# Windowed value rows read once into SBUF, the overlap between windows copied on chip

## The chip, the cores and the metric

The kernel runs on one core of one Trainium2 chip. The metric is device time in microseconds (us) of that core; lower is better. Five engines work side by side, each with its own instruction stream that it executes in order: PE (TensorE, matmuls), DVE (VectorE), ACT (ScalarE), POOL (GpSimd) and SP (SyncE, which here only issues transfers). POOL, SP and ACT issue DMA transfers, each into a queue of its own; all of them are moved by the core's 16 DMA engines. An engine that reaches an instruction with a wait stands still until the wait is met.

## The reference

Two layers are computed one after the other.

```
# 1. chunked attention; B=4, H=8, S=768, D=64, 8 memory rows per head
for c in range(S // 32):                      # 24 chunks of 32 query rows
    window = rows [32c-16, 32c+40) of k and v, cut at 0 and S     # up to 56 rows
    k_full = concat(mem_k, k[window]);  v_full = concat(mem_v, v[window])
    out[chunk c] = softmax(scale * q_c @ k_full.T) @ v_full
# 2. x = out as [3072, 512]; 8 experts, F = 1024, top 2 by noisy logits
logits = x @ w_gate + log1p(exp(x @ w_noise)) * noise
y[token] = sum over its 2 best experts e of weight * relu(x @ w1[e]) @ w2[e]
```

Neighbouring windows overlap: rows 32 to 55 of the window of chunk c are rows 0 to 23 of the window of chunk c+1.

## The kernel before

**Stages.** An attention stage covers about the first 137 us of the profiled execution, with the top-2 routing woven in. From about 144 us on comes the expert stage, in which PE runs the experts' two matmuls over gathered tiles of 128 tokens (`mm1` L705, `mm2` L723) and results are scattered to DRAM (`put` L676). The expert stage can begin only when the last tile's routing is known.

**Tiling of attention.** A loop (L562) runs over 12 tiles t = 0 to 11, three for each of the 4 batches (`b, tp = divmod(i, TP)`). A tile is 256 tokens, in two halves of 128, with all 8 heads. Step i computes the scores of tile i+1 (`scores` L402: PE, then DVE for the maximum L423 and the subtraction L425), transposes the probabilities of tile i (`turn_p` L433: PE, then the ACT copy `pT` L439), stores the attention output of the batch before (`keep_x` L484, at tp = 0, issued from ACT's queue), transposes the output of tile i-1 (`turn_x` L466: PE, then the ACT copy `xT` L472), multiplies probabilities by values (`values` L442, PE L453, then DVE L460), takes the exponential for tile i+1 (`exps` L428, ACT L430), and computes the gate of tile i-1 (`gate` L475). PE, ACT, DVE and SP follow this hand-written order; on POOL the pinned instructions keep the program's order too.

**The values' way.** For each batch, `load_v` brings v into the SBUF buffer `vn` (cast to bf16), `spread_v` (L366, two POOL copies) reorders it into `vp`, and `window_v` (L372) does the rest. SP writes `vp` to a DRAM scratch `vd` (L374), padded by zero rows. POOL then issues two small transfers of the memory rows (L378) and four that read the windows back from `vd` (L383). The result `vb` holds, at each of 64 partitions of a half, one row of the window for all 24 chunks. The two halves of 64 partitions carry even and odd heads. In the buffer before, partitions 0 to 7 of a half hold memory rows and 8 to 63 the 56 window rows, read as rows 0 to 31 and rows 32 to 55. There are two `vb` buffers; batch b uses `vb[b % 2]`.

**What shares a tensor.** `vn`, the two `vb`, the buffers `nat` for the loaded k and q, and `xrow` (the attention output that `keep_x` stores) are all column ranges of one big SBUF tensor, `w_all`, which later holds the experts' weights. The program's planner derives waits between instructions from the regions of a tensor that they read and write.

**Order of POOL's queue.** For batch b+1, at step tp = 0 of batch b, POOL issues in this order: memory rows and windows of batch b+1 (L568), the loads of q and k of batch b+2 (L570), `spread_v(b + 2)`, and the load of v of batch b+3 (L573). Before the loop come v, k, q of batch 0, the windows of batch 0 (L528), then v, q, k of batch 1, its spread, and v of batch 2. The weights of experts 0 to 2 follow at steps 6 to 8.

Of the kernel before, what the change touches and what calls it, by code (L numbers as in the profile page):

```python
# [18 lines left out]
NEG = -1e30  # L19
# [3 lines left out]
def kernel(  # L23
# [24 lines left out]
    HP = H // 2  # L48
# [4 lines left out]
    NCH = S // CH  # L53
# [16 lines left out]
    def pin(i):  # L70
        tc.keep_in_program_order(i)
# [32 lines left out]
    def scratch(n):  # L104
        scol[0] -= n
        return wflat[:, scol[0]:scol[0] + n]
    xrow = [scratch(SO * Dm).rearrange("p (s r) -> p s r", s=SO) for _ in range(2)]
    vn = scratch(H * SO * D).rearrange("p (h c) -> p h c", h=H)
    vb = [scratch(2 * NCH * HP * D).rearrange("p (a c w) -> p a c w", a=2, c=NCH) for _ in range(2)][::-1]
    nat = [[scratch(H * SO * D).rearrange("p (h c) -> p h c", h=H) for _ in range(2)] for _ in range(2)]  # L110
    assert scol[0] >= 2 * WE
    mvs = w_all[0:B * NM, 0, 0:2 * H * D].bitcast(F32).rearrange("p (h d) -> p h d", h=H)
# [52 lines left out]
    mvn = keep.tile([B * NM, Dm], BF16, name="mvn")  # L165
# [53 lines left out]
    kT = keep.tile([128, HP, 2, SP], BF16, name="kT")  # L219
    qT = [keep.tile([128, HP, S], BF16, name=f"qT{i}") for i in range(2)]  # L220
    for par in range(2):
        nc.scalar.copy(vb[1][own(par), 1 - par].rearrange("p (x c) w -> p x (c w)", x=NCH // 2),
                       zeros[own(par), :].unsqueeze(1).to_broadcast([64, NCH // 2, Dm]))

    mkT = keep.tile([128, HP, 2, B * NM], BF16, name="mkT")
# [146 lines left out]
    def window_v(b):  # L372
        t, o = vb[b % 2], vd[b % 2]
        nc.sync.dma_start(out=o[LC:LC + S, :].rearrange("(p s) c -> p (s c)", s=SO), in_=vp)  # L374
        for par in range(2):
            p0 = par * 64
            cols = slice(par * 256, (par + 1) * 256)
            pin(nc.gpsimd.dma_start(out=t[p0:p0 + NM, par], in_=mvn[b * NM:(b + 1) * NM, cols].unsqueeze(1).to_broadcast([NM, NCH, 256])))  # L378
        for par in range(2):
            p0 = par * 64  # L380
            cols = slice(par * 256, (par + 1) * 256)
            for r0, n in ((0, CH), (CH, WIN - CH)):
                pin(nc.gpsimd.dma_start(out=t[p0 + NM + r0:p0 + NM + r0 + n, par],  # L383
                                        in_=o[r0:r0 + S, cols].rearrange("(c k) w -> k c w", k=CH)[0:n]))


    def turn(b, unit):
# [14 lines left out]
    def scores(t):  # L402
        b, tp = divmod(t, TP)
        ps_s = psS.tile([128, 2, HP, 2, KW], F32, name="ps_s")
        for j in range(2):
            for pair in range(HP):
                tk = (2 * tp + j) * 128
                nc.tensor.matmul(out=ps_s[:, j, pair, :, 0:NM], lhsT=qT[b % 2][:, pair, tk:tk + 128],
                                 rhs=mkT[:, pair, :, b * NM:(b + 1) * NM], start=True, stop=True)
        for j in range(2):  # L410
            for pair in range(HP):
                tk = (2 * tp + j) * 128
                for r in range(4):
                    tr = tk + r * CH
                    nc.tensor.matmul(out=ps_s[r * CH:(r + 1) * CH, j, pair, :, NM:KW], lhsT=qT[b % 2][:, pair, tr:tr + CH],  # L415
                                     rhs=kT[:, pair, :, tr:tr + WIN], start=True, stop=True, tile_position=(0, r * CH))
        if tp == 0:
            nc.vector.memset(ps_s[0:CH, 0, :, :, NM:NM + LC], NEG)
        if tp == TP - 1:
            nc.vector.memset(ps_s[128 - CH:128, 1, :, :, KW - RC:KW], NEG)  # L420
# [95 lines left out]
    with tc.manual_schedule(engines={ET.PE, ET.Activation, ET.DVE, ET.SP}):  # L516
# [5 lines left out]
        for par in range(2):  # L522
            nc.vector.tensor_copy(mkT[own(par), :, par, :], p_mk[own(par)].rearrange("p c x b m -> p c (x b m)"))
        for par in range(2):
            nc.vector.memset(vb[0][own(par), 1 - par], 0.0)
# [35 lines left out]
        r0, ra, rb, rc = Route(0, 6, 8), Route(6, 8, 8), Route(14, 6, 8), Route(20, 4, 4)  # L561
        for i in range(NT):  # L562
            b, tp = divmod(i, TP)
# [22 lines left out]
            if not last:  # L586
                sc = scores(i + 1)
# [291 lines left out]
    for i, (b, e, s0, ds_, n, ps_) in enumerate(steps):  # L879
        if i == 0:  # L880
# [5 lines left out]
            s0, n = 1, 2  # L886
# [11 lines left out]
        for pr in ps_:  # L898
            k = pairs.index(pr)
            x = pr.index(e)  # L900
# [8 lines left out]
        if i == 9:  # L909
# [3 lines left out]
            dstx, _, wx = next(dx), next(dx), next(dx)  # L913
# [21 lines left out]
    with tc.manual_schedule(engines={ET.Pool}):  # L935
        nov = nc.values_load(nxt[0:1, 0:1], min_val=0, max_val=NX,
                             skip_runtime_bounds_check_because="computed on chip from counts that sum to the tokens")
        with tc.If(nov > 1):
            for t in range(1, NX):
# [3 lines left out]
                dstx, _, wx = next(dx), next(dx), next(dx)  # L943
# [42 lines left out]
```

## Time and profile before

| what | value |
|---|---|
| median of 3 runs | 362.4 us (360.43 to 364.03) |
| the profiled execution's own time | 358.42 us |
| its span, and mean granted TensorE clock | 356.7 us, 0.867 |
| PE, DVE, ACT, POOL busy | 80%, 48%, 38%, 38% of the span |
| window reads L383 | 8 of 384 KB and 8 of 288 KB, median 13.0 and 13.3 us from issue to landing |
| writes of `vd` L374 | 4 of 768 KB, median 9.0 us |
| loads of v, k, q | 4 each of 768 KB, median 12.1, 20.9, 18.1 us |

Lines such as L383 are lines of the kernel before. "Landing" is when a transfer's completion arrives. A line of the timeline gives start, duration, engine, line, operation, how many instructions were merged (x8), and in square brackets how long the engine was idle before and whose completion ended that idle time. A letter q after an engine's name marks the engine's instruction queue (its sequencer) rather than its compute part.

### The profile page before, as it was taken

The page shows a single profiled execution, that of the slowest core. Times are in us where ns is not written, and L with a number is a line of the kernel's source. Part 1 is how long each engine was busy: PE and PEld are TensorE (multiplying, and loading weights), DVE is VectorE, ACT ScalarE, POOL GpSimd, SP SyncE. Part 2 cuts the span into 40 slices and gives each one's busy share as a digit, 9 for nine tenths or more (in the row PEclk, how much of TensorE's full clock was granted, in tenths as well). Part 3 has the DMA queues.
Part 4 walks back from the last instruction along what each step waited for, and adds up shares of the span by engine and source line. Part 5 has one row for each costly group of instructions (what it writes and reads, how often), then busy time and mean ns, then how long its engine had stood idle before and what let it go on. Part 6 is the DMA issues. An engine that isn't in the chain of part 4 may idle for free.

```text
span 356.7 us, 7042 instructions
## 1 busy us (share of the span) xinstructions
PE 285.9 (80%) x2934; PEld 186.3 (52%) x2955; DVE 170.3 (48%) x349; ACT 136.9 (38%) x189; POOL 134.3 (38%) x181
## 2 busy tenths in 40 slices
PE   0356577777847732999999999999999999999991
PEld 0245455666736621865544465664455775565540
DVE  7656456699689885531133302954310334223221
ACT  8813645564645610144322343213243222243310
POOL 6460573354453036706530744332580122201122
PEclk9995655565687865699999999999999999999998
DMA  8999999999999999499999999961289971100012
GB/s 122 235 171 169 245 174 208 251 198 211 247 156 208 253 249 180 106 194 143 178 196 235 209 173 252 159 119 51 87 166 189 208 184 54 53 2 2 25 47 81
DMA packets 49866, 56.97 MB, mean 160 GB/s; under 512 B 16931, under 2 KB 39523, under 8 KB 49828
## 3 DMA queue, kind: packets, MB, share of 16 engines
q0 software_dynamic: 34240, 46.82, 73.2%
q1 hardware_dynamic: 13920, 6.62, 10.9%
q10 hardware_dynamic: 1668, 3.02, 2.4%
q8 instruction: 25, 0.41, 0.5%
q14 instruction: 13, 0.11, 0.1%
HBM read 70.39 MB, written 13.96 MB: 236 GB/s over the span
## 4 chain that ended last, share of the span: by engine, by line
PE 33%; issue 20%; POOL 5%; DVE 4%; DMA 3%; POOLq 1%; ACT 0%; DVEq 0%
PE p_h L714 18%; PE p_y L726 13%; POOL out_dram L677 4%; DMA out_dram<-y,main_dst 1%; DMA xTt<-xt 1%; DMA xt<-xd,main_src 1%; POOL xt L671 1%; DVE w_all L460 1%; PE p_xt L691 0%; POOL w_all L844 0%; POOLq L981 0%; DVE mx L423 0%; DVE sc L425 0%; ACT xT L472 0%; PE ps_o L453 0%
## 5 line engine op out<-in xcount | busy, mean ns | idle before, releaser
L714 PE MATMUL p_h<-xTt,w_all 128*128 128x256 bf16 (+3 forms) x669 | 102.7, 313 | 0.7 <-DVE xTt L692 0.5
L726 PE MATMUL p_y<-w_all,h 128*128 128x512 bf16 x446 | 102.3, 379 | 0.9
L714 PEld LDWEIGHTS <-w_all 128*128 128x128 bf16 x736 | 70.0, 101 | 36.3 <-issue 0.7
L702 ACT ACTIVATE h<-p_h 128x512 bf16<-128x512 f32 (+1 forms) x81 | 44.7, 551 | 95.9 <-PE p_h L714 88.3
L726 PEld LDWEIGHTS <-h 128*128 128x128 bf16 x464 | 45.3, 98 | 51.6
L700 DVE TENSOR_SCALAR h<-p_h 128x512 bf16<-128x512 f32 (+1 forms) x49 | 31.0, 633 | 82.8 <-PE p_h L714 73.7
L677 POOL DMA_INDIRECT out_dram<-y,main_dst x28 | 30.9, 1103 | 87.9 <-DVE y L732 75.4
L732 DVE SCALAR_TENSOR_TENSOR y<-p_y,main_w,y 128x512 f32<-128x512 f32 x28 | 21.0, 750 | 39.2 <-PE p_y L726 32.5
L393 PE MATMUL p_t<-identb,w_all 128*64 128x128 bf16 x384 | 20.6, 288 | 23.0 <-DMA w_all<-in_k_dram 13.4
L671 POOL DMA_INDIRECT xt<-xd,main_src x28 | 27.9, 997 | 24.2 <-DMA xTt<-xt 13.0
L730 ACT ACTIVATE y<-p_y,main_w 128x512 f32<-128x512 f32 x28 | 19.2, 687 | 37.0 <-PE p_y L726 36.0
L393 PEld LDWEIGHTS <-w_all 128*64 128x64 bf16 x384 | 18.1, 155 | 25.2 <-DMA w_all<-in_k_dram 13.9
L439 ACT COPY pT<-p_p 128x1024 bf16<-128x1024 bf16 x12 | 12.1, 1012 | 27.5 <-PE p_p L436 27.5
L383 POOL DMA_DIRECT2D w_all<-vd x16 | 11.8, 747 | 23.8 <-DMA vd<-vp 19.3
L460 DVE TENSOR_TENSOR w_all<-ps_o,rs 128x512 bf16<-128x512 f32 x24 | 15.6, 686 | 8.2 <-PE ps_o L453 7.8
L415 PE MATMUL ps_s<-kT,qT 128*32 128x112 bf16 x384 | 11.6, 276 | 7.2 <-DVE kT L549 5.4
L368 POOL COPY vp<-w_all 128x1536 bf16<-128x1536 bf16 x8 | 11.5, 1469 | 13.2 <-DMA w_all<-in_v_dram 13.2
L430 ACT ACTIVATE pb<-sc 128x1024 bf16<-128x1024 f32 x12 | 12.8, 1063 | 8.9 <-DVE sc L425 8.7
L549 DVE COPY kT<-p_t 64x768 bf16<-64x768 bf16 x12 | 11.5, 955 | 7.9 <-PE p_t L393 7.8
L425 DVE TENSOR_TENSOR sc<-ps_s,mx 128x1024 f32<-128x1024 f32 x12 | 14.7, 1225 | 0.8
L423 DVE TENSOR_REDUCE mx<-ps_s 128x16 f32<-128x1024 f32 x12 | 14.7, 1224 | 0.8 <-PE ps_s L415 0.5
L453 PE MATMUL ps_o<-w_all,pT 128*32 128x128 bf16 x384 | 10.9, 280 | 3.3 <-issue 2.0
(172 smaller groups left out, 284.0 us busy)
## 6 DMA issues: line engine op xcount, KB each, us to landing
w_all<-in_moe_w_dram POOLq DMA_DIRECT2D x16, 1024.0 KB, 20.7
w_all<-in_moe_w_dram POOLq DMA_DIRECT2D x8, 512.0 KB, 13.8
w_all<-in_v_dram POOLq DMA_DIRECT2D x4, 768.0 KB, 12.1
w_all<-in_k_dram POOLq DMA_DIRECT2D x4, 768.0 KB, 20.9
w_all<-in_q_dram POOLq DMA_DIRECT2D x4, 768.0 KB, 18.1
vd<-vp SPq DMA_DIRECT2D x4, 768.0 KB, 9.0
w_all<-vd POOLq DMA_DIRECT2D x8, 384.0 KB, 13.0
w_all<-vd POOLq DMA_DIRECT2D x8, 288.0 KB, 13.3
```

The costliest lines, as they stand in the source:

```text
L393: nc.tensor.transpose(out=p_t[own(par), s, :], in_=src[:, 2 * pair + par, s * D:(s + 1) * D], identity=identb, tile_position=(0, par * 64))
L423: nc.vector.tensor_reduce(out=mx, in_=s3, axis=AX, op=Alu.max)
L425: nc.vector.tensor_tensor(out=sc, in0=s3, in1=bc(mx, KW), op=Alu.subtract)
L460: nc.vector.tensor_tensor(out=xr[:, j, 0:Dm].rearrange("p (h d) -> p h d", h=H), in0=ps_o[:, j].rearrange("p c a d -> p (c a) d"), in1=bc( ...
L671: i = nc.gpsimd.indirect_dma_start(out=xts[key].bitcast(I32), out_offset=None, in_=xd, in_offset=bass.IndirectOffsetOnAxis(ap=ix, axis=0))
L677: i = nc.gpsimd.indirect_dma_start(out=out, out_offset=bass.IndirectOffsetOnAxis(ap=ix, axis=0), in_=y, in_offset=None, bounds_check=N - 1 ...
L700: nc.vector.tensor_scalar(out=out_, in0=in_, scalar1=0.0, scalar2=None, op0=Alu.max)
L702: nc.scalar.activation(out=out_, in_=in_, func=Act.Relu)
L714: nc.tensor.matmul(out=o, lhsT=w(kp * F + f * 128, 128), rhs=x[:, kp], start=(kp == 0), stop=(kp == KP - 1))
L726: nc.tensor.matmul(out=p, lhsT=h[:, (f * n + j) * 128:(f * n + j + 1) * 128], rhs=w(KP * F + f * Dm, Dm), start=(f == 0), stop=(f == FB - 1))
L730: nc.scalar.activation(out=y, in_=p, func=Act.Copy, scale=weight)
L732: nc.vector.scalar_tensor_tensor(out=y, in0=p, scalar=weight, in1=y, op0=Alu.mult, op1=Alu.add)
```

## The change

The 64 partitions of a half of `vb` are now ordered as 56 window rows and then 8 memory rows; scores, masks and the memory transfer follow that order. `vb` has 25 chunk places instead of 24. Window rows 0 to 31 are read from `vd` for 25 chunks, by eight transfers per batch: for r = 0 to 3 and for each half, the eight rows r, r+4, ..., r+28, which go to every fourth partition. Rows 32 to 55 are no longer read from DRAM: SP's queue copies them from partitions 0 to 23, one chunk further on, one transfer for each half.

```
-    vb = [scratch(2 * NCH * HP * D).rearrange("p (a c w) -> p a c w", a=2, c=NCH) ...
+    vb = [scratch(2 * (NCH + 1) * HP * D).rearrange("p (a c w) -> p a c w", a=2, c=NCH + 1) ...
...
         for par in range(2):
-            pin(nc.gpsimd.dma_start(out=t[p0:p0 + NM, par], in_=mvn[...]...to_broadcast([NM, NCH, 256])))
+            pin(nc.gpsimd.dma_start(out=t[p0 + WIN:p0 + KW, par, 0:NCH],
+                                    in_=mvn[...]...to_broadcast([NM, NCH, 256])))
+        for r in range(4):
+            for par in range(2):
+                p0 = par * 64
+                cols = slice(par * 256, (par + 1) * 256)
+                pin(nc.gpsimd.dma_start(out=t[p0 + r:p0 + CH:4, par],
+                                        in_=o[:, cols].rearrange("(c k r) w -> r k c w", k=CH // 4, r=4)[r]))
         for par in range(2):
             p0 = par * 64
-            cols = slice(par * 256, (par + 1) * 256)
-            for r0, n in ((0, CH), (CH, WIN - CH)):
-                pin(nc.gpsimd.dma_start(out=t[p0 + NM + r0:p0 + NM + r0 + n, par],
-                                        in_=o[r0:r0 + S, cols].rearrange("(c k) w -> k c w", k=CH)[0:n]))
+            nc.sync.dma_start(out=t[p0 + CH:p0 + WIN, par, 0:NCH].rearrange("p c w -> p (c w)"),
+                              in_=t[p0:p0 + WIN - CH, par, 1:NCH + 1].rearrange("p c w -> p (c w)"))
...
-                nc.tensor.matmul(out=ps_s[:, j, pair, :, 0:NM], ...
+                nc.tensor.matmul(out=ps_s[:, j, pair, :, WIN:KW], ...
...
-                    nc.tensor.matmul(out=ps_s[r * CH:(r + 1) * CH, j, pair, :, NM:KW], ...
+                    nc.tensor.matmul(out=ps_s[r * CH:(r + 1) * CH, j, pair, :, 0:WIN], ...
```

The two masks (L418, L420) and the zeroing of `vb` (L222, L525) move by the same shifts.

More of the change, by code (lines that the diff above doesn't have):

```diff
@@ L108 @@
     vn = scratch(H * SO * D).rearrange("p (h c) -> p h c", h=H)
-    vb = [scratch(2 * NCH * HP * D).rearrange("p (a c w) -> p a c w", a=2, c=NCH) for _ in range(2)][::-1]
+    vb = [scratch(2 * (NCH + 1) * HP * D).rearrange("p (a c w) -> p a c w", a=2, c=NCH + 1) for _ in range(2)][::-1]
     nat = [[scratch(H * SO * D).rearrange("p (h c) -> p h c", h=H) for _ in range(2)] for _ in range(2)]
@@ L221 @@
     for par in range(2):
-        nc.scalar.copy(vb[1][own(par), 1 - par].rearrange("p (x c) w -> p x (c w)", x=NCH // 2),
+        nc.scalar.copy(vb[1][own(par), 1 - par, 0:NCH].rearrange("p (x c) w -> p x (c w)", x=NCH // 2),
                        zeros[own(par), :].unsqueeze(1).to_broadcast([64, NCH // 2, Dm]))
@@ L377, in window_v @@
             cols = slice(par * 256, (par + 1) * 256)
-            pin(nc.gpsimd.dma_start(out=t[p0:p0 + NM, par], in_=mvn[b * NM:(b + 1) * NM, cols].unsqueeze(1).to_broadcast([NM, NCH, 256])))
+            pin(nc.gpsimd.dma_start(out=t[p0 + WIN:p0 + KW, par, 0:NCH],
+                                    in_=mvn[b * NM:(b + 1) * NM, cols].unsqueeze(1).to_broadcast([NM, NCH, 256])))
+        for r in range(4):
[4 more added lines that the diff above has]
+                                        in_=o[:, cols].rearrange("(c k r) w -> r k c w", k=CH // 4, r=4)[r]))
         for par in range(2):
             p0 = par * 64
-            cols = slice(par * 256, (par + 1) * 256)
-            for r0, n in ((0, CH), (CH, WIN - CH)):
-                pin(nc.gpsimd.dma_start(out=t[p0 + NM + r0:p0 + NM + r0 + n, par],
-                                        in_=o[r0:r0 + S, cols].rearrange("(c k) w -> k c w", k=CH)[0:n]))
+            nc.sync.dma_start(out=t[p0 + CH:p0 + WIN, par, 0:NCH].rearrange("p c w -> p (c w)"),
+                              in_=t[p0:p0 + WIN - CH, par, 1:NCH + 1].rearrange("p c w -> p (c w)"))
     def turn(b, unit):
@@ L407, in scores @@
                 tk = (2 * tp + j) * 128
-                nc.tensor.matmul(out=ps_s[:, j, pair, :, 0:NM], lhsT=qT[b % 2][:, pair, tk:tk + 128],
+                nc.tensor.matmul(out=ps_s[:, j, pair, :, WIN:KW], lhsT=qT[b % 2][:, pair, tk:tk + 128],
                                  rhs=mkT[:, pair, :, b * NM:(b + 1) * NM], start=True, stop=True)
@@ L414, in scores @@
                     tr = tk + r * CH
-                    nc.tensor.matmul(out=ps_s[r * CH:(r + 1) * CH, j, pair, :, NM:KW], lhsT=qT[b % 2][:, pair, tr:tr + CH],
+                    nc.tensor.matmul(out=ps_s[r * CH:(r + 1) * CH, j, pair, :, 0:WIN], lhsT=qT[b % 2][:, pair, tr:tr + CH],
                                      rhs=kT[:, pair, :, tr:tr + WIN], start=True, stop=True, tile_position=(0, r * CH))
         if tp == 0:
-            nc.vector.memset(ps_s[0:CH, 0, :, :, NM:NM + LC], NEG)
+            nc.vector.memset(ps_s[0:CH, 0, :, :, 0:LC], NEG)
         if tp == TP - 1:
-            nc.vector.memset(ps_s[128 - CH:128, 1, :, :, KW - RC:KW], NEG)
+            nc.vector.memset(ps_s[128 - CH:128, 1, :, :, WIN - RC:WIN], NEG)
         s3 = ps_s.rearrange("p j c a w -> p (j c a) w")
@@ L524 @@
         for par in range(2):
-            nc.vector.memset(vb[0][own(par), 1 - par], 0.0)
+            nc.vector.memset(vb[0][own(par), 1 - par, 0:NCH], 0.0)
         nc.vector.tensor_copy(mvn.rearrange("m (a c d) -> m a c d", a=2, c=HP), mvs.rearrange("m (c a) d -> m a c d", a=2))
```

## The prediction

> **What bounds the kernel now.** The page first, then the stretches of the expert stage.
>
> ```profile
> PE 285.9 (80%) x2934; PEld 186.3 (52%) x2955; DVE 170.3 (48%) x349; ACT 136.9 (38%) x189; POOL 134.3 (38%) x181
> ...
> DMA  8999999999999999499999999961289971100012
> ```
> ```profile
> 160.00:180.00 20.00, 19.89 (x108) 10.62 (x109) 4.08 (x8) 8.15 (x15) 12.03 (x13) 1.00 1.06 163
> ```
>
> From 144 us on PE has no gap (19.89 of 20 us busy, clock 1.00), so whatever moves that stage's start moves the end by as much. Before it, the 16 DMA engines are full (16 slices of 8.9 us, 143 us, all but the first at 9) and PE is not. So I read the attention stage through its transfers. The timeline of POOL, which issues nearly all of them:
>
> ```profile
> 19.97 2.96 POOL L383 DMA_DIRECT2D w_all<-vd  x4 [4.95 <-DMA vd<-vp]
> 22.92 0.94 POOL L117 DMA_DIRECT2D w_all<-in_v_dram  x1
> 23.83 0.92 POOL L117 DMA_DIRECT2D w_all<-in_q_dram  x1
> 24.72 0.90 POOL L117 DMA_DIRECT2D w_all<-in_k_dram  x1
> 35.95 2.88 POOL L368 COPY vp<-w_all 128x1536 bf16<-128x1536 bf16 x2 [10.34 <-DMA w_all<-in_v_dram]
> ...
> 45.77 2.96 POOL L383 DMA_DIRECT2D w_all<-vd  x4 [4.42 <-issue]
> 48.72 0.92 POOL L117 DMA_DIRECT2D w_all<-in_q_dram  x1
> ```
>
> To see: right behind the four window reads the next loads are issued, so POOL's queue always holds a backlog, and its transfers land in the order of issue. The queue is what feeds PE and POOL. Now ACT around the first `keep_x` (L485), and PE behind it:
>
> ```profile
> 57.68 1.01 ACT L439 COPY pT<-p_p 128x1024 bf16<-128x1024 bf16 x1 [1.99 <-PE p_p L436]
> 57.76 0.37 ACTq L485 DMA_DIRECT2D xd<-w_all  x1
> 58.59 1.02 ACT L472 COPY xT<-p_x 128x1024 bf16<-128x1024 bf16 x1
> 59.49 1.07 ACT L430 ACTIVATE pb<-sc 128x1024 bf16<-128x1024 f32 x1
> ...
> 87.14 1.01 ACT L439 COPY pT<-p_p 128x1024 bf16<-128x1024 bf16 x1 [3.02 <-PE p_p L436]
> 87.22 0.34 ACTq L485 DMA_DIRECT2D xd<-w_all  x1
> 88.05 1.02 ACT L472 COPY xT<-p_x 128x1024 bf16<-128x1024 bf16 x1
> ```
> ```profile
> 68.03 1.49 PE L393 MATMUL p_t<-identb,w_all 128*64 128x128 bf16 x24 [2.63 <-DMA w_all<-in_q_dram]
> ```
>
> To see: ACT passes each `keep_x` at once, and its next copies follow within 1 us.
>
> **The change: what goes.** Per batch, 1,088 of 2,688 row pieces of 512 B are no longer read. The trace's landings give a full set after the memory rows 9.3 us (windows of batch 2: 77.5 to 86.9; of batch 3: 99.4 to 108.7), so 1,600 pieces are worth 5.5 us: 3.8 us less of queue per batch. POOL issues eight reads instead of four; at 0.72 us each (L383 takes 0.73 to 0.77, the smaller L378 0.67) that is 5.8 us instead of 2.96. The two copies of 24 x 12 KB on SP's queue are not in the trace. A 6 KB packet takes 247 ns and an engine gets few 12 KB rows, so 1 us of transfer; a small transfer (the gathers L671) lands 2.8 to 3 us after issue, the larger `vd` write 7.2 us. I take 3, between 2.8 and 7.2. Scores and masks only shift columns: nothing, as forms and counts stay.
>
> **What is added: waits.** The built program's own list of waits shows what the diff does not. The planner takes a write to every fourth partition as touching other columns of `w_all` too, so these appear, between buffers that share no byte:
> - window reads wait for the k, q and v loads issued before them (`nat`, `vn`);
> - the load of v (batch 1) and of q (batches 2, 3) waits for all eight window reads before it to land; behind it on POOL stand the other loads, the spread, the next windows;
> - `keep_x` of batches 0 and 1, on ACT, waits for all eight window reads of batch 2 and 3. Behind it on ACT stand the copy `xT` L472, the exponential L430 and the next `pT` L439; PE waits for each (gate, `turn_p`, `values`).
>
> The backlog that hid every transfer's latency is thus gone; how far 3.8 us per batch pays for it has to be added up.
>
> *POOL's chain, in us of the profiled execution.* A set of windows lands 8.3 after its start (seven issues of 0.72, then 3 for the last, small one). A load into an empty queue lands 8.1 after issue (v of batch 0: 1.5 to 9.6), one behind another +4.3 (k of batch 0: 9.56 to 13.84), or +5.9 where `vd` is written beside it (k of batch 1: 39.7 to 45.6).
> - windows 0 start at 20.3 (q of batch 0 lands 20.28; before 19.97), land 28.6 (before 32.7).
> - v1 28.6 + 8.1 = 36.7; q1 41.0; k1 46.9; v2 51.2 (before 35.9, 39.7, 45.6, 50.3).
> - windows 1 start at 51.2 (before 45.8), land 59.5, copied 62.5 (before 60.8).
> - q2 67.6; k2 73.5 beside the write of `vd`; v3 77.8 (before 68.0, 71.8, 76.2).
> - windows 2 start at 77.8, land **86.1** (before 86.9).
>
> So loads and windows come within about 2 us of where they came. This part alone costs about nothing: the saving pays for the lost backlog.
>
> *ACT's first hold.* The compute is about 1 us late by 58, so ACT arrives at `keep_x` at 58.8 and stands until 86.1. Then `xT` at 86.5, exponential to 88.4, scores (L415) and transposes on PE to 90.1, `pT` at 90.0 (before 64.59, +25.4). There the wait for q of 2.63 us (the PE line above) is gone, since q2 and k2 have landed: +22.9. From there to the next `keep_x` I see no idle time of PE put down to a transfer, so it keeps: `pT` at 110.0, `keep_x` reached at 110.1.
>
> *ACT's second hold.* The windows of batch 3 overwrite the buffer that `values` of tile 5 reads, and come behind POOL's `vals` (L342, before 81.84 to 83.66). That wait is old and hidden; now tile 5 is late. Its last values come at 81.9 + 22.9 = 104.8, `vals` ends by 106.0, memory rows 1.35, windows 3 start near 107 and land at 115.5. ACT goes on there: `xT` at 115.8 against 88.05, +27.7. Of this 0.3 comes back at q3 (PE idle 0.33). The 1.4 us idle at k3 does not come back: DVE, with the routing's `choose` and then the `kT` copies until 105.6, ends later there. The third `keep_x` waits for no window. Windows and copy 3 are landed by 119, before tile 9 needs them. Experts 0 and 1 follow by about 140, and expert 2, issued once `nat` is read (near 127), by about 150; the stage that needs them starts near 171.
>
> Sum: **+27 us** at the start of the expert stage, nothing after. On the profiled 358.4 us that is 385; this execution is 4.0 us under the median of 362.4 (360.4 to 364.0), and from the median it is 389. I give 388.
>
> **A rule against the change.** The nearest row for the new reads is the pair of memory-row transfers (eight partitions, one per half): issued 0.7 us apart, landed 21.52 and 21.89, and in batch 1 51.51 and 51.84, so the two overlap. The Trainium skill, DMA: Bandwidth & Descriptors, section Rules for kernel authors, says that transfers to two disjoint partition halves serialize and should be one transfer. By that rule the sum would be that of the second rival; the trace disagrees so far, in pairs of the same eight partitions.
>
> **The rivals.**
> 1. *PE and ACT catch up after the holds.* Everything loaded waits ready, and the clock in 50 to 70 us was granted at 0.50; at 1.00 a `turn_p` takes 0.62 instead of 1.03 us (both in the timeline). For: the stretch from 110 to 120 was at 0.91. Against: the clock is low where PE has gaps, and it keeps them. PE is busy 30 us in 60 to 100 (6.22, 7.98, 7.69 and 8.16 per 10 us, granted 0.50 to 0.76); a quarter of that, some 8 us, could go: +27 - 8 = +19, 381.
> 2. *Eight-partition reads do not overlap.* 25 pieces per engine at 9.3 x 16 / 2,688 = 55 ns are 1.4 us; eight in a row 11.1 us, a set 5.6 us longer than above. Three sets stand before the first hold's end and one before the second's: +27 + 22 = +49, 411. Against it: the pair above.
> 3. *Faster: the queue is all that matters.* If `keep_x` found its windows landed, ACT would not hold, and 3.8 us per batch would bring k of batch 3 (98.5 before) some 11 us earlier; half of that is lost to DVE's `choose`, leaving 5 to 8: 355. It decides at L485: windows 2 would have to land by 58.8, 27 us earlier than added up, though q2, k2 and v3 stand before them. Only waits that the program does not really carry would do it.
> 4. *Within 1%:* the hold is covered by waits that ACT would have had anyway. In 58 to 86 ACT's own waits on transfers are under 3 us; little.
>
> **How the numbers follow.** Forecast 0.74; rival 1 0.12; rival 2 0.06; rival 3 0.05; rival 4 0.03. The forecast's unknowns: the copies (up to +4 each, on no chain but beside q2 and v1), a set of windows 7.5 to 10, a load 7.5 to 9.5: the first hold ends between 81 and 97. That is 383 to 399; with 2 to 3 us for the second set and rival 1's 381, itself 5 us uncertain, 376 to 402; rivals 2, 3 and 4 are left out. A measurement of this kernel tells about 1% from no change (its three runs span 1%). Slower by over 1%: 0.74 + 0.12 + 0.06 = 0.92; within 0.03; faster 0.05.
>
> **What would show it.** In the changed kernel's profile: an idle of about 25 us on ACT before an `xT` copy, ended by window reads from `vd`, and a second of 4 to 7 us; two slices of PE near 0 at 65 to 86; the DMA row with digits under 9 in the first 100 us; v1 issued near 28.6, not 22.9; the first expert matmul (L714) near 171 instead of 144.14, and from there to the end the same 213 us. I am wrong if ACT passes L485 without a wait, if a set of windows takes over 10 us, or if the expert stage waits for weights.

## The result, and the profile after

The changed kernel takes 399.0 us (median of four runs, 397.6 to 400.4) against 361.6 us for the kernel before (360.4 to 364.0, measured beside it): a ratio of 1.103, with a 95% interval of 1.098 to 1.107. The prediction was 388 us, slower, with a range of 376 to 402. The profiled execution took 398.95 us, its span 397.2 us (before: 358.42 and 356.7). The profiled execution of before is thus 3.2 us faster than the median of its kernel, that of after is at its median; the two profiles differ by 40.5 us where the medians differ by 37.4.

First the page of the kernel after: busy shares, then PE and DMA in 40 slices of 9.9 us.

```profile
PE 284.2 (72%) x2955; PEld 183.3 (46%) x2955; DVE 169.9 (43%) x349; ACT 136.7 (34%) x189; POOL 143.2 (36%) x197
...
PE   0366483004552665437999999999998999999991
...
DMA  9949967957957999505999999996139991100012
```

PE does the same work (284.2 us busy, 285.9 before) in a longer span. Slices 7 and 8 of PE (counted from 0), 69.5 to 89.4 us, are nearly empty. The DMA row, full for 16 slices before, now has digits of 4 to 7 among the first 13: the queue runs dry although the kernel reads less (68.16 MB from HBM, 70.39 before).

The timeline of POOL shows why. L384 are now the window reads; they were L383.

```profile
21.00 5.20 POOL L384 DMA_DIRECT2D w_all<-vd  x8 [5.99 <-DMA w_all<-in_q_dram]
29.02 0.92 POOL L117 DMA_DIRECT2D w_all<-in_v_dram  x1 [2.83 <-DMA w_all<-vd]
...
39.08 2.88 POOL L368 COPY vp<-w_all 128x1536 bf16<-128x1536 bf16 x2 [7.37 <-DMA w_all<-in_v_dram]
...
53.97 5.17 POOL L384 DMA_DIRECT2D w_all<-vd  x8 [9.53 <-DMA w_all<-in_v_dram]
62.56 0.93 POOL L117 DMA_DIRECT2D w_all<-in_q_dram  x1 [3.42 <-issue]
...
85.11 5.17 POOL L384 DMA_DIRECT2D w_all<-vd  x8 [15.38 <-DMA w_all<-in_v_dram]
92.89 0.92 POOL L117 DMA_DIRECT2D w_all<-in_q_dram  x1 [2.61 <-DMA w_all<-vd]
```

In the square brackets two waits alternate that the kernel before did not have: window reads wait for a load (`in_q_dram`, `in_v_dram`), and the next load waits for the window reads (`vd`). Before, the loads followed the reads at once (22.92 behind 19.97). The line at 62.56 names no transfer as releaser ("issue"), but in the trace it too waits for the counters of these reads.

Now ACT around the first two `keep_x` (L490):

```profile
60.42 1.01 ACT L444 COPY pT<-p_p 128x1024 bf16<-128x1024 bf16 x1 [1.99 <-PE p_p L441]
92.47 0.37 ACTq L490 DMA_DIRECT2D xd<-w_all  x1
92.94 1.01 ACT L477 COPY xT<-p_x 128x1024 bf16<-128x1024 bf16 x1 [31.51 <-DMA w_all<-vd]
...
114.48 1.01 ACT L444 COPY pT<-p_p 128x1024 bf16<-128x1024 bf16 x1 [0.83 <-PE p_p L441]
124.98 0.34 ACTq L490 DMA_DIRECT2D xd<-w_all  x1
125.42 1.01 ACT L477 COPY xT<-p_x 128x1024 bf16<-128x1024 bf16 x1 [9.93 <-issue]
```

ACT's sequencer stands at `keep_x` until 92.47 and again until 124.98, and ACT is idle for 31.5 and 9.9 us before the copies `xT` behind it. The last line names no releaser, but here too the trace has `keep_x` wait for the counters of all eight reads. The list of waits of the attention stage shows who pays:

```profile
PE small L485 <- ACT xT L477: 37.4, 3, 26.5
...
PE ps_o L458 <- DMA w_all<-w_all: 6.8, 2, 4.6
```

PE stands 37.4 us for `xT`, and 6.8 us more for the on-chip copies (`w_all<-w_all`), a wait that the prediction did not have. The first expert matmul comes at 178.59 us, against 144.14: +34.45 of the 40.5 us by which the span grew. The rest is lost in the expert stage. Its stretches, start to end, length, then PE busy, and in the last three columns the granted clock, DMA share and GB/s; first after, then before:

```profile
177.50:189.20 11.70, 9.18 (x70) 7.80 (x71) 4.31 (x13) 1.48 (x4) 8.46 (x10) 0.65 0.52 117
195.00:215.00 20.00, 20.00 (x112) 10.76 (x111) 4.56 (x8) 7.84 (x15) 10.20 (x11) 1.00 1.05 167
```
```profile
143.00:149.40 6.40, 5.85 (x49) 5.43 (x50) 3.52 (x12) 0.85 (x2) 5.40 (x7) 0.50 0.37 106
```

Full clock begins for good 11.7 us after the stage's start, not 6.4, with 2.5 us of gaps in that stretch where there were 0.6. After this stretch PE is as full as before but for one wait of 1.4 us.

### The profile page after: what moved, and what is told of

It is laid out like the page before. It is cut to its first block, busy times and chain, and to the rows that moved or that the text cites. A ratio compares the mean times of both kernels' runs of the same rounds, so it can differ in the third digit from the quotient of the medians.

```text
span 397.2 us, 7122 instructions
## 1 busy us (share of the span) xinstructions
PE 284.2 (72%) x2955; PEld 183.3 (46%) x2955; DVE 169.9 (43%) x349; ACT 136.7 (34%) x189; POOL 143.2 (36%) x197
## 3 DMA queue, kind: packets, MB, share of 16 engines
HBM read 68.16 MB, written 13.96 MB: 207 GB/s over the span
## 4 chain that ended last, share of the span: by engine, by line
PE 30%; issue 20%; DVE 4%; POOL 4%; DMA 1%; POOLq 1%; ACT 0%; DVEq 0%
PE p_h L719 16%; PE p_y L731 12%; POOL out_dram L682 3%; DMA out_dram<-y,main_dst 1%; DVE w_all L465 1%; PE p_xt L696 1%; PE p_list L352 1%; POOL w_all L849 0%; DVE mx L428 0%; DVE sc L430 0%; POOLq L986 0%; ACT xT L477 0%; PE ps_o L458 0%; DVE xTt L697 0%; DVE vals L342 0%
## 5 line engine op out<-in xcount | busy, mean ns | idle before, releaser
L719 PE MATMUL p_h<-xTt,w_all 128*128 128x256 bf16 (+3 forms) x672 | 103.9, 315 | 2.5 <-issue 2.0
L731 PE MATMUL p_y<-w_all,h 128*128 128x512 bf16 x464 | 103.9, 379 | 1.4 <-ACT y L735 1.4
L676 POOL DMA_INDIRECT xt<-xd,main_src x28 | 28.0, 999 | 22.6 <-DMA xTt<-xt 11.3
L398 PE MATMUL p_t<-identb,w_all 128*64 128x128 bf16 x384 | 20.1, 283 | 21.1 <-DMA w_all<-in_k_dram 11.5
L485 PE MATMUL small<-wgn,xT 128*128 128x16 bf16 x96 | 4.3, 172 | 42.9 <-ACT xT L477 37.4
L384 POOL DMA_DIRECT2D w_all<-vd x32 | 20.7, 653 | 33.0 <-DMA w_all<-in_v_dram 24.9
L477 ACT COPY xT<-p_x 128x1024 bf16<-128x1024 bf16 x12 | 12.2, 1016 | 43.8 <-DMA w_all<-vd 31.5
L485 PEld LDWEIGHTS <-xT 128*128 128x128 bf16 x96 | 3.7, 100 | 44.4 <-ACT xT L477 38.3
L435 ACT ACTIVATE pb<-sc 128x1024 bf16<-128x1024 f32 x12 | 12.7, 1061 | 10.0 <-DVE sc L430 10.0
L487 DVE COPY lg_all<-small 128x32 f32<-128x32 f32 x12 | 2.2, 184 | 32.6 <-PE small L485 32.6
L420 PE MATMUL ps_s<-kT,qT 128*32 128x112 bf16 x384 | 11.1, 273 | 5.7 <-DVE kT L554 5.2
```

The source lines that it names most:

```text
L384: pin(nc.gpsimd.dma_start(out=t[p0 + r:p0 + CH:4, par], in_=o[:, cols].rearrange("(c k r) w -> r k c w", k=CH // 4, r=4)[r]))
L398: nc.tensor.transpose(out=p_t[own(par), s, :], in_=src[:, 2 * pair + par, s * D:(s + 1) * D], identity=identb, tile_position=(0, par * 64))
L435: nc.scalar.activation(out=pb.rearrange("p x a w -> p (x a) w"), in_=sc, func=Act.Exp, scale=scale)
L676: i = nc.gpsimd.indirect_dma_start(out=xts[key].bitcast(I32), out_offset=None, in_=xd, in_offset=bass.IndirectOffsetOnAxis(ap=ix, axis=0))
L719: nc.tensor.matmul(out=o, lhsT=w(kp * F + f * 128, 128), rhs=x[:, kp], start=(kp == 0), stop=(kp == KP - 1))
L731: nc.tensor.matmul(out=p, lhsT=h[:, (f * n + j) * 128:(f * n + j + 1) * 128], rhs=w(KP * F + f * Dm, Dm), start=(f == 0), stop=(f == FB - 1))
```

## The experiments

All runs are given as a ratio to the kernel before in the same series (361.99 to 362.55 us). Times are medians; the profile of a run shows one execution of it. The theory after the result: (1) the waits that a write to every fourth partition creates cost most of it, by ACT's holds and by POOL's chain; (2) the eight reads and the copies cost something by themselves. The rivals: the transfers themselves (their number, their shape, the copies) cost most, and the waits only show it.

### ACT's holds taken away

`keep_x` is issued from SP's queue, so that its wait for the window reads holds nothing of ACT's.

```
-                keep_x(b - 1, 0, SO, nc.scalar)
+                keep_x(b - 1, 0, SO, nc.sync)
```

> The changed kernel with the two stores of the attention output of batches 0 and 1 issued from SP's queue instead of ACT's; SP stands there anyway, since its copies wait for the same window reads. Theory (the loss is ACT held at these stores): both idles of ACT, 31.5 and 9.9 us, go. What stays is POOL's chain of loads and windows, which in the changed kernel ran late by up to 10 us (q and k of batch 3 issued at 92.9, landing near 108 instead of 98.5), so about 373 us, 366 to 380. Rival (the late transfers alone set the time, ACT would wait elsewhere): 392 to 400.

Measured: 381.96 us, ratio 1.055 (1.047 to 1.063). 17 us come back, fewer than the theory's 19 to 33. ACT now passes:

```profile
60.38 1.01 ACT L444 COPY pT<-p_p 128x1024 bf16<-128x1024 bf16 x1 [1.98 <-PE p_p L441]
61.28 1.02 ACT L477 COPY xT<-p_x 128x1024 bf16<-128x1024 bf16 x1
```

But right behind the hold stands another wait. The copies of batch 2 on SP's queue, and PE's value matmul that needs them:

```profile
93.16 1.66 SPq L388 DMA_DIRECT2D w_all<-w_all  x2
```
```profile
104.05 1.04 PE L458 MATMUL ps_o<-w_all,pT 128*32 128x128 bf16 x32 [11.64 <-DMA w_all<-w_all]
```

The copies are issued at 93.16, as the window reads of that batch land, and PE gets its rows 11 us later. So the hold was real, but of the 37.4 us that PE stood for `xT` only 17 come back: behind it the windows and their copies were late anyway. In the profiles, 12.7 of the 16.5 us are gained before the expert stage (its first transpose comes at 164.83, not 177.49), the rest in it.

### The same reads without a stride

Eight reads of eight rows as in the change, to eight neighbouring partitions each, in place of every fourth. The bytes, the row pieces and the number of transfers are the same; the added waits go.

```
-                pin(nc.gpsimd.dma_start(out=t[p0 + r:p0 + CH:4, par],
-                                        in_=o[:, cols].rearrange("(c k r) w -> r k c w", k=CH // 4, r=4)[r]))
+                pin(nc.gpsimd.dma_start(out=t[p0 + 8 * r:p0 + 8 * r + 8, par],
+                                        in_=o[:, cols].rearrange("(c r k) w -> r k c w", k=CH // 4, r=4)[r]))
```

> The changed kernel with the eight reads taking eight neighbouring rows each (rows 0 to 7, 8 to 15, ...) instead of every fourth: the same number of reads, bytes and pieces, the same copies, but no write to every fourth partition, and so none of the added waits. Theory (the waits are the whole loss, the smaller reading is a small gain): 352 to 364 us, against 361.6 before. Rival A (eight small transfers and the copies cost by themselves): 375 to 395. Rival B (partition stride itself is slow in the DMA engines): also near 360, but then a set of windows lands in clearly less than the 7.5 us of the changed kernel when the queue is empty.

Measured: 370.67 us, ratio 1.025 (1.017 to 1.034): between the two. ACT passes both `keep_x` at once. All the waits that the stride creates are thus worth 28 of the 37 us, 17 on ACT and 11 more on POOL. The remaining 8 us stay with eight reads and copies. Rival B, a stride that is slow in the DMA engines, can't be read from this run, since its loads now run beside the reads; in the changed kernel the strided reads landed at the pace of their issue, which speaks against it. POOL's timeline of this run, in the third set of windows, and PE's list of waits:

```profile
76.36 0.65 POOL L384 DMA_DIRECT2D w_all<-vd  x1 [0.83 <-DMA w_all<-in_k_dram]
83.06 1.30 POOL L384 DMA_DIRECT2D w_all<-vd  x2 [6.05 <-DMA w_all<-in_v_dram]
```
```profile
PE ps_o L458 <- DMA w_all<-w_all: 12.8, 2, 7.6
PE ps_o L458 <- DMA w_all<-in_q_dram: 8.6, 1, 8.6
```

The fifth to eighth read of this set wait in the middle of it for loads and memory rows that touch none of their bytes. The built program counts POOL's transfers on eight counters in turn, and one batch now has 13 of them (three loads, two of memory rows, eight reads), so a read waits for the transfer that used its counter before; the trace shows these waits at just these counters.

### The strided reads kept, the copies taken away

Rows 32 to 55 are read from DRAM again, as in the kernel before, behind the eight strided reads.

```
-            nc.sync.dma_start(out=t[p0 + CH:p0 + WIN, par, 0:NCH].rearrange("p c w -> p (c w)"),
-                              in_=t[p0:p0 + WIN - CH, par, 1:NCH + 1].rearrange("p c w -> p (c w)"))
+            cols = slice(par * 256, (par + 1) * 256)
+            pin(nc.gpsimd.dma_start(out=t[p0 + CH:p0 + WIN, par, 0:NCH],
+                                    in_=o[CH:CH + S, cols].rearrange("(c k) w -> k c w", k=CH)[0:WIN - CH]))
```

> The changed kernel without the copies on SP's queue: rows 32 to 55 are read from the DRAM scratch again by the two transfers of the kernel before, behind the eight strided reads. The added waits stay but name the eight strided reads alone. Theory (waits are the loss; copies are off every chain): 1,088 pieces per batch come back, 3.8 us in each of three sets before the first hold ends, less what their landing is not waited for: 396 to 412 us. Rival (the copies' 12 KB packets, 850 ns each, starve the loads behind them and are part of the loss): 385 to 396, and the three loads of q, k and v of batches 2 and 3 take under 20 us instead of 22.5.

Measured: 391.13 us, ratio 1.077 (1.070 to 1.084). The time is the rival's: with 1,088 more row pieces to read per batch the kernel is 8 us faster than the changed one. The load of v of batch 1 is issued at 28.75 and has landed by the first of these lines, q, k of batch 2 and v of batch 3 are issued from 61.51 on and have landed by the second:

```profile
36.31 2.88 POOL L368 COPY vp<-w_all 128x1536 bf16<-128x1536 bf16 x2 [4.87 <-DMA w_all<-in_v_dram]
...
81.58 5.18 POOL L384 DMA_DIRECT2D w_all<-vd  x8 [12.87 <-DMA w_all<-in_v_dram]
```

That is 7.6 us for the one load (10.1 in the changed kernel, 29.02 to 39.08) and 20.1 for the three (22.5, 62.56 to 85.11), just over the rival's 20. So the copies, although on a queue of their own, delay the loads behind them, here by more than the reads that they replace, and POOL's chain waits for those loads. But this explains only a part of the 8 us. The first gain is gone at the next set, which starts at 53.51 against 53.97; ACT's holds end 2.3 and 2.2 us earlier (90.14 and 122.76); and the expert stage starts only 0.7 us earlier (176.75 against 177.49). Of the 5.5 us between the two profiled spans, 4.8 lie inside the expert stage, and why was not tried.

### One read per half, copies kept

The change without its stride and without its eight transfers: one read of 32 neighbouring rows by 25 chunks for each half, then the copies on SP's queue.

```
-        for r in range(4):
-            for par in range(2):
+        for par in range(2):
...
+                pin(nc.gpsimd.dma_start(out=t[p0:p0 + CH, par],
+                                        in_=o[:, cols].rearrange("(c k) w -> k c w", k=CH)))
```

> The kernel before with only the idea of the change: one read of 32 neighbouring rows and 25 chunks per half (two reads per batch instead of eight or four), rows 32 to 55 copied on chip by SP's queue. No strided write, so no added waits, and half of POOL's issues gone. Theory: POOL's queue saves up to 3.8 us per batch, of which the routing and the copies' latency leave little: 350 to 360 us against 361.6. Rival (the copies' way is longer than what the reads save, PE waits for them): 362 to 372.

Measured: 363.22 us, ratio 1.002 (0.998 to 1.007): the kernel before, to the resolution of the measurement. The saved reading buys nothing here, and the PE timeline of this run shows what takes at least part of it:

```profile
38.12 1.04 PE L457 MATMUL ps_o<-w_all,pT 128*32 128x128 bf16 x32 [6.41 <-DMA w_all<-w_all]
65.67 1.04 PE L457 MATMUL ps_o<-w_all,pT 128*32 128x128 bf16 x32 [5.76 <-DMA w_all<-w_all]
```

The copies of batch 0 are issued from 26.72 on; PE has its rows at 38.12. In the kernel before the same matmul ran at 32.79.

### One read per half, rows 32 to 55 left out

The copies are dropped, and rows 32 to 55 of the windows are zeros, so the values of these rows are missing from the output (and, as the fill reached too far, the memory rows of batch 0).

> As the kernel with one read of 32 neighbouring rows per half (363.2 us, same as before), but the two on-chip copies per batch are left out: rows 32 to 55 of every window stay zero, written once by POOL in gaps of its own, and the values of these rows are left out of the output. Theory: the 1,088 row pieces per batch that are no longer read are worth 3.8 us of queue per batch, and the copies give them back, since the value matmuls waited 6.4, 5.8 and 1.6 us for them in batches 0 to 2. Then this kernel takes 348 to 357 us, the first p_xt comes near 132 to 138 us, and no value matmul waits over 3 us for a write into the windows. Rival: the queue is not what bounds these stages, and the waits for copies only stood where another wait would: 359 to 366 us.

Measured: 357.53 us, ratio 0.985 (0.978 to 0.993). The first transposes of the expert stage:

```profile
137.01 0.59 PE L698 MATMUL p_xt<-identb,xt 128*128 128x128 bf16 x4 [1.60 <-DMA xt<-xd,main_src]
```

They come 7.9 us earlier than with copies (144.88) and 6.0 earlier than before (143.04). The fill did not lie in a gap: POOL's two fills waited for the memory rows and ran from 21.55 to 26.85, and the first window reads were issued 5.3 us later than with copies. The time lies 0.5 us above the theory's range, its other two signs hold (137.01, and no value matmul waits over 2.5 us). So 357.5 bounds from above what the kernel would take if the rows came for nothing, and the copies give back at least 5.7 us.

### Four reads

Two reads of 16 neighbouring rows for each half, copies as before: nine POOL transfers per batch.

```
+        for r in range(2):
+            for par in range(2):
...
+                pin(nc.gpsimd.dma_start(out=t[p0 + 16 * r:p0 + 16 * r + 16, par],
+                                        in_=o[:, cols].rearrange("(c r k) w -> r k c w", k=CH // 2, r=2)[r]))
```

> Two reads of 16 neighbouring rows per half, no stride, copies as before: four reads per batch, between the two (363.2 us) and the eight (370.7 us) of neighbouring rows. Theory: what eight reads cost over two is the number of completion lanes, eight for POOL's transfers: with three loads, two rows of memory values and eight reads a batch has 13, with two reads 7, with four 9. So four reads wait once and cost nearly nothing, 362 to 365.5 us. Rival: the cost goes with the time to issue and to read, 0.7 us a transfer, evenly: 365.5 to 369 us.

Measured: 373.14 us, ratio 1.027 (1.019 to 1.035). Both expectations fail: four reads are not cheaper than eight (370.67). The waits for counters are there with nine transfers as well, at loads now, the longest first. The kernel before has nine transfers per batch too (four reads), and its loads wait for the same counters, as the two lines below show:

```profile
81.61 0.88 POOL L117 DMA_DIRECT2D w_all<-in_k_dram  x1 [6.66 <-DMA w_all<-in_v_dram]
```
```profile
72.11 0.92 POOL L117 DMA_DIRECT2D w_all<-in_q_dram  x1 [2.96 <-DMA w_all<-in_k_dram]
76.45 0.90 POOL L117 DMA_DIRECT2D w_all<-in_k_dram  x1 [3.42 <-DMA w_all<-in_v_dram]
```

So nine transfers alone don't make a kernel slow. And the expert stage of the run with four reads starts at 148.93, only 4.1 us later than with two (144.88). The other 6 us go in that stage: 222.4 us from its first transpose to the end of the span, against 216.2. It holds one wait of 3.5 us that the run with two reads has with 1.3:

```profile
275.24 5.30 PE L731 MATMUL p_y<-w_all,h 128*128 128x512 bf16 x16 [3.54 <-ACT y L735]
```

Behind that wait the granted clock was 0.50 for 3.4 us (276.1 to 279.5), with 1.00 on both sides. Why this stage differs was not settled. So the number of reads has a price of some 4 to 10 us over two, but the counters alone don't give it.

### The copy on VectorE

One read per half; the copies are made by VectorE, ahead of each tile's value matmuls.

```
+            for par in range(2):
+                p0 = par * 64
+                nc.vector.tensor_copy(vb[b % 2][p0 + CH:p0 + WIN, par, 8 * tp:8 * tp + 8]...,
+                                      vb[b % 2][p0:p0 + WIN - CH, par, 8 * tp + 1:8 * tp + 9]...)
```

> As the kernel with one read of 32 neighbouring rows per half, but rows 32 to 55 are copied by VectorE, two copies of 24 partitions x 2,048 elements ahead of the value matmuls of each tile (24 in all), in place of the two copies per batch on SyncE's queue. Theory: what gives the saved reading back is the landing of the copies by DMA, 6 to 11 us. VectorE is busy 168 us of 361; copies of 1 to 2 us each, estimated from 0.95 us for 64x768 and 2.6 us for a 64x3072 fill, put 2 to 4 us on each of 12 tiles, some of it in gaps. Then 350 to 360 us. Rival: VectorE becomes the bound of the attention tiles, 362 to 378 us, with VectorE busy over 90% of the slices up to the first expert.

Measured: 376.86 us, ratio 1.040 (1.032 to 1.049). The time is the rival's, its reason only in part: VectorE's digits up to the first expert are 5 to 8, not over 9, and a copy is short (median 685 ns). But it stands in the chain of every tile, behind the maximum and the subtraction of the next tile's scores:

```profile
PE ps_o L453 <- DVE w_all L599: 30.9, 12, 5.4
```

PE waits 12 times, 2.6 us each. An engine that is half idle can still be late at each single step.

### Copies in thirds

One read per half; each copy on SP's queue is cut into three of eight chunks, the first tile's first.

```
-            nc.sync.dma_start(out=t[p0 + CH:p0 + WIN, par, 0:NCH]..., in_=t[p0:p0 + WIN - CH, par, 1:NCH + 1]...)
+        for tp in range(TP):
+            for par in range(2):
+                p0 = par * 64
+                nc.sync.dma_start(out=t[p0 + CH:p0 + WIN, par, 8 * tp:8 * tp + 8]...,
+                                  in_=t[p0:p0 + WIN - CH, par, 8 * tp + 1:8 * tp + 9]...)
```

> As the kernel with one read of 32 neighbouring rows per half, but each copy on SyncE's queue is cut into three of eight chunks (4,096 bytes in one piece in place of 12,288), the ones that the first tile of a batch needs first. Theory: the copies are late because of their size and of what they share the DMA engines with; the first tile then waits only for a third of the bytes, its wait of 6.4 us in batch 0 and 5.8 in batch 1 falls to under 4, and the time is 354 to 361 us. Rival: the delay lies in the order of the transfers (loads that were issued ahead of the copies are served first), not in their size: the waits stay over 5 us and the time is 361 to 368 us.

Measured: 359.18 us, ratio 0.988 (0.981 to 0.995): faster than the kernel before by about 1%, little but clear of the noise. PE's list of waits for the attention stage:

```profile
PE ps_o L458 <- DMA w_all<-w_all: 9.0, 3, 5.2
```

13.8 us of waits have become 9.0: 2.6 in batch 0 (6.4 with whole copies), 5.2 in batch 1 (5.8), 1.1 in batch 2 (1.6). The theory holds for batch 0 and for the time, and not for batch 1. There q and k of batch 2 and v of batch 3 were issued 0.5 to 9 us ahead of the copies, as the rival has it; that this order is the reason was not tried.

### The first tile's rows read, the rest copied

As in thirds, but rows 32 to 55 of the first eight chunks are read from DRAM by SP's queue, behind its write of `vd`.

```
+        for par in range(2):
+            p0 = par * 64
+            cols = slice(par * 256, (par + 1) * 256)
+            nc.sync.dma_start(out=t[p0 + CH:p0 + WIN, par, 0:8],
+                              in_=o[CH:CH + 8 * CH, cols].rearrange("(c k) w -> k c w", k=CH)[0:WIN - CH])
-        for tp in range(TP):
+        for tp in range(1, TP):
```

> As the kernel with copies in thirds (359.2 us, 0.988 of before), but rows 32 to 55 of the first eight chunks, which the first tile of a batch needs, are read from DRAM by SyncE's queue right behind its write of the value rows, and only the chunks of the second and third tile are copied on chip. Theory: the copies in thirds still leave 9 us of waits (2.6, 5.2 and 1.1) since the copy can only start when the window reads have landed; these reads can start with them, 384 row pieces per batch of the 1,088 that are saved. The waits fall under 2 us each, 354 to 358.5 us. Rival: the reads are served as late as the copies, behind POOL's loads, or delay those, and nothing is gained: 358.5 to 364 us.

Measured: 358.22 us, ratio 0.987 (0.981 to 0.993). No value matmul waits for a window any more by the profile. That of the first tile of batch 0 comes at 31.71 without a wait; that of batch 1 has one that the profile can't name:

```profile
57.00 1.05 PE L463 MATMUL ps_o<-w_all,pT 128*32 128x128 bf16 x32 [1.59 <-issue]
```

From the version in thirds (0.988) it can't be told apart by its time.

### All rows read, rows 32 to 55 by SP's queue

The control for the last two: no copies, all the reading of the kernel before, only the issuing queue differs.

```
+            nc.sync.dma_start(out=t[p0 + CH:p0 + WIN, par, 0:NCH],
+                              in_=o[CH:CH + S, cols].rearrange("(c k) w -> k c w", k=CH)[0:WIN - CH])
```

> All window rows are read from DRAM again, as before, and nothing is copied on chip; but the reads of rows 32 to 55 are issued by SyncE's queue and not by POOL's. Theory: what the kernel with copies in thirds wins is the reading that it saves (the kernel without rows 32 to 55 takes 357.5 us, that with one copy per half 363.2), so with all the reading the time is that of before, 360.5 to 366 us. Rival: what counts is only that POOL issues two window reads per batch and not four (1.5 us in place of 3, and two completions fewer), wherever the rest comes from: 355 to 360 us.

Measured: 363.37 us, ratio 1.001 (0.996 to 1.006). Issuing from another queue wins nothing by itself, which fits the theory that the versions with copies in thirds win by the reading that they save. The separation is not clean, since here PE waits long for SP's reads of batch 1:

```profile
64.95 1.05 PE L458 MATMUL ps_o<-w_all,pT 128*32 128x128 bf16 x32 [8.29 <-DMA w_all<-vd]
```

## Why the prediction was right, and where it was off

**The mechanism was right.** The waits that it read from the built program (window reads for loads, loads for window reads, `keep_x` for window reads) are in the trace at their places, and the run without the stride shows them worth 28 of 37 us. ACT's first hold ran from 60.5 to 92.5 (forecast 58.8 to 86.1), its second from 114.6 to 125.0 (110.1 to 115.5). PE's two empty slices, the DMA row's low digits and ACT's two idle times came as announced. The loads follow the windows (v of batch 1 at 29.02, forecast 28.6). A full set of eight reads took 8.0 us (21.00 to 29.02) and 8.6 (53.97 to 62.56) until the next load was issued, as forecast with 8.3. The last set took 11.0 us until `keep_x` passed (114.00 to 124.98), over the 10 that the prediction named as a sign of being wrong: its last two reads were issued late, as told below. PE's waits in the expert stage name no weights.

**Rival 2's price, some 14 us for a set, is excluded:** the trace shows eight transfers of eight partitions done in 8.0 to 8.6 us. The Trainium skill (DMA: Bandwidth & Descriptors, section Rules for kernel authors) says that transfers to disjoint partition halves serialize. Whether they do is not decided here: the reads are issued 0.65 us apart and land at about that pace, so one after the other fits as well. Nor did the pair of memory rows decide it, against the prediction's reading. 96 KB landing 0.37 us behind another 96 KB is some 265 GB/s, and the engines moved 281 GB/s in the stretch from 60 to 70 us of the same profile, so these two can also have gone one after the other.

**The terms that were mis-sized** are two. The first is *the copies on SP's queue*, "on no chain" and 3 us until they land, a price taken from the quickest gathers (2.8 to 3 us; the median of the 28 is 4.0). In the changed kernel's trace they land 4.0 to 10.1 us after their issue. They are 192 packets of 12,288 bytes with a median of 850 ns, on 12 of the 16 engines; a 6,144-byte packet of the `vd` write takes 247 ns, and from that row "1 us of transfer" had been worked out. They cost in three places. PE waits 6.8 us for them in the changed kernel, 2.2 of it in batch 0, where the same matmul came 1.9 us later than before (34.69 against 32.79); ACT came to its first hold 1.7 us later than forecast (the other 4.6 lie inside that hold). The three loads issued beside the copies of batch 1 took 22.5 us (q, k of batch 2 and v of batch 3), against 20.1 without the copies and a forecast of 18.3. And they are what stood behind ACT's hold when it was taken away.

The second is *a load behind another*, forecast with +4.3, or +5.9 beside the write of `vd`. In the run without the copies, v of batches 2 and 3 landed 5.4 us after the k before it, and k of batches 1 and 2 landed 6.8 and 6.3 us after q. The four loads from v of batch 1 to v of batch 2 took 24.9 us with the copies and 24.8 without, where 22.6 were counted. Both together send the end of the first hold from 86.1 to 92.5; without the copies, and with more to read, it ended at 90.1.

**The second hold** was 10.4 us and not 5.4. The memory rows of batch 3 were issued at 112.67, after PE's values of tile 5, 6.7 us later than added up; most of that is the first hold's delay handed on. Then the eight reads needed until 125.0, 12.3 us after the memory rows where 9.5 were counted, since the last two stood 0.9 and 1.2 us for memory rows to land, a wait for a counter.

**The sum to the expert stage**, in us, with the second `keep_x` reached 0.1 us after the start of its `pT`, as in the trace of before:

| step | forecast | measured | difference |
|---|---|---|---|
| end of the first hold | 86.1 | 92.5 | +6.4 |
| from there to the second `keep_x` | 24.0 | 22.1 | -1.9 |
| second hold | 5.4 | 10.4 | +5.0 |
| from there to the first expert matmul | 55.6 | 53.6 | -2.0 |
| first expert matmul | 171.1 | 178.6 | +7.5 |

That the first matmul came within 7.5 us is in part luck: two errors of 5 to 6 us late and two of 2 us early. PE and ACT did catch up a little, 2 us in each of two stretches, not the 8 of rival 1.

**"Nothing after" was off by 6 us.** From its first transpose to the end the expert stage took 219.7 us, not 213.7. The stretches above show its start: 2.5 us of gaps and a later full clock; a wait of 1.4 us for ACT's `y` at 303.5 and the tail make up the rest. The 213.7 come from an execution that was 3.2 us faster than its median, so a part of the 6 may be the difference between executions. In the other profiles the stage takes between 214.5 (reads without a stride) and 222.4 us (four reads). What sets it was not tried.

**"This part alone costs about nothing"**, said of POOL's chain, was wrong when it stands alone. With ACT's holds gone, POOL's added waits still cost 11 us (381.96 to 370.67). The saved reading is worth at least 5.0 us in all (362.5 to 357.5, the run without rows 32 to 55).

**Where the 37 us are:** ACT's holds 17, POOL's other added waits 11, eight reads instead of two 7.5, and under 1 for what is left, the copies having eaten the reading saved. By the start of the expert stage in the profiles, the same steps are 12.7, 10.5, 9.4 and 1.8 of 34.4 us; the rest of the first two arises in the expert stage. These are steps in one order; in another the shares would differ, as waits lie behind waits.

## What to carry to other kernels

A transfer that writes every fourth partition of a shared tensor can be planned as a write to everything between, and then waits appear between buffers that share no byte; read them off the built program before counting bytes. Write neighbouring partitions, or give such a target a tensor of its own (not tried here).

A copy on chip by DMA is no free replacement for a read: it can start only when its source has landed, and it shares the DMA engines with the loads beside it. Copy in pieces, those of the first consumer first, and the saved reading shows as about 1% of the time (359.2 against 362.5 us); reading the first consumer's rows directly did no better that could be measured (358.2 against 362.0 us).

## What the runs showed of the hardware

**Shorter rows made a copy on chip cheaper.** The run with one read per half and the version in thirds differ in the cut of the copies alone. Whole copies are 192 packets of 12,288 bytes there, median 691 ns, 138 us summed over the engines; thirds are 576 packets of 4,096 bytes, median 172 ns, 114 us in all. Length alone is not the reason: in the changed kernel packets of 12,288 bytes took from 460 ns (27 bytes per ns, against 24 of a 4,096-byte packet at its median) to 1,694 ns. What slows most of them was not tried.

**A transfer of 24 partitions uses 12 of the 16 engines.** The Trainium skill (DMA: Bandwidth & Descriptors, section Why a DMA increments its semaphore by 16 and not by 1) says that the number of engines is the largest up to 16 that divides the slowest dimension of source and target; 24 gives 12. The trace agrees: a copy's counter goes up once early and 12 times as it lands, that of the write of `vd` from 128 partitions 16 times. The Trainium skill (DMA: Bandwidth & Descriptors, section Queues, rings and completion order) says that an engine takes turns between queues packet by packet. No run here isolates that: the three loads behind the copies of batch 1 took 22.5 us with these and 20.1 without, the four before them 24.9 and 24.8.

**POOL's transfers meet at eight counters in these programs.** In the traces each transfer of POOL uses the counter of the eighth one before it, and waits until that one has landed. In the lines above that is 3.42 us in the kernel before, 6.05 with eight reads and 6.66 with four.
